# A linear-attention and sine-gated layer on one core: the opening with v in four loads, w1 issued behind them, and all v scaled by GpSimd

## The chip, the cores and the metric

One core of a Trainium2 chip runs the whole kernel. The metric is the device time in microseconds of one execution. Lower is better.

## The reference

Attention with a decay per head, over blocks, and then a two-layer network on the result (cut to what matters):

```python
# attention: q, k, v are [4, 8, 768, 64]; lam is [8]
for b in range(nb):                                  # blocks of 64 positions
    intra = einsum('bhic,bhjc->bhij', qb, kb) * Dmask        # lam**(i - j), i >= j
    intra = einsum('bhij,bhjd->bhid', intra, vb)
    inter = einsum('bhid,bhde->bhie', qb * lam_pow, kv_state)
    out[:, :, sl] = intra + inter
    kv_state = lam_block * kv_state + einsum('bhsd,bhse->bhde', kb * rev_pow, vb)

# network: x is the attention result as [3072, 512]
h = x @ w_in                                         # [3072, 2048]
g = h + sin(alpha * h)**2 / (alpha + 1e-9)
return g @ w_out                                     # [3072, 512]
```

## The kernel before

**Tiles and steps.** The kernel works on blocks of 128 positions. Two batch rows (`u` = 0, 1) share the 128 partitions, 64 each, and one step is one block of 128 positions of such a pair for four of the eight heads. There are 24 steps: two pairs of rows, 6 blocks and 2 halves of the heads. Steps 0 and 1 are the two head halves of block 0, steps 2 and 3 those of block 1. Four steps make 512 columns of x, one chunk of the network; there are six chunks.

**What one step does** (function `sec`). A step passes through three stages, each of which can be given to `sec` by the step's number:

- `t`: 32 TensorE transposes of q and k (L481) into PSUM, and one evacuation to `qkT` (L666) on the engine named in `t_engs`.
- `s`: 16 matmuls for the scores (L493), and their product with the causal mask into `S_m` (`put_S`, L611 on VectorE straight from PSUM; with `via`, ScalarE first copies the scores to `S_raw`, L607, and VectorE multiplies from there, L608).
- `o`: the output (L505 within the block, L515 with the state) and the state's increment (L528). `put_O` then evacuates the output times a decay table into `xT` (L624, VectorE), copies the first state for the next block to `Zs` (L634, ScalarE), and keeps the running state in `Zacc` (L629 the first time, L645 later).

The decay is carried by tables: v is scaled by `Lv` before use (`prep_v`, L460, v32 to v2, on GpSimd or VectorE), and x by `Xt` (L411) when it is evacuated.

**The network.** `grp_A` (L683) makes one 128-row slice of h for one chunk with four matmuls, ScalarE takes its sine (L687), one of three engines squares it (L694 or L695), and VectorE joins it with h into gT (L697). `grp_B` (L720) multiplies gT with w_out. Chunk 0's `grp_A` starts when x of steps 0 to 3 is complete; the attention of later steps is laid between the later matmuls.

**What sets the order.** The lines L758 to L895 record every operation with its engine and an estimated duration (`rec`, which is `Program.add`). The planner gives each one a start time: TensorE and SyncE in the order of recording, VectorE, ScalarE and GpSimd in the first gap that is long enough. DMA issues occupy their engine (0.75 us on GpSimd, less for small ones), and their landing is estimated from `nbytes`. Each engine then runs its operations in the order of these start times, and waits on semaphores for what they depend on. Readers of one PSUM bank on different engines are also put in the order of recording (L90 to L92). So a changed estimate can change an order, but not what is computed.

**The opening before.** k and q of blocks 0 and 1 are issued first (GpSimd, 8 loads of 128 KB). Then come transposes of steps 0 and 1, the mask tables (`consts2`), v of blocks 0 and 1 in eight loads of half the heads each (`by_step`, 128 KB), scores of steps 0 and 1, transposes of 2 and 3, and the scaling of step 0 on GpSimd. The first block of w1 is held back until that scaling is done. Then come scores of step 2, the scaling of step 1 on VectorE, the output of step 0 with the scores of step 3 ahead of its evacuation, the output of step 1, scalings of steps 2 and 3 on GpSimd, the last two w1 blocks behind them, and the outputs of steps 2 and 3. The Sin table load (L426) is recorded late, but the planner puts it in an early gap of ScalarE.

The PSUM banks of the opening: outputs of step 0 use banks 4 and 5, which its scores held, of step 1 banks 6 and 7, of steps 2 and 3 banks 0 to 3.

Of the kernel before, what the change touches and what calls it, by code (L numbers as in the profile page):

```python
# [187 lines left out]
def bass_lightning_attn__then__act_snake_kernel(  # L188
# [15 lines left out]
    NB = S // BL  # L204
# [5 lines left out]
    HS = 4  # L210
# [11 lines left out]
    with es:  # L222
        def sb(name, shape, dt):
            return es.enter_context(nc.sbuf_tensor(name, shape, dt))
# [28 lines left out]
        maskf = sb("maskf", [128, 256], F32)  # L253
# [6 lines left out]
        Lv = sb("Lv", [128, NB, H, 2], F32)  # L260
# [10 lines left out]
        junk = sb("junk", [128, 1], F32)  # L271
# [4 lines left out]
        P = Program()  # L276
# [19 lines left out]
        def half(r):  # L296
            return slice(64 * r, 64 * r + 64)

        def where(s):
            pair, n, hh = s // 12, (s % 12) // 2, s % 2  # L300
            return pair, n, hh

        def load(d, x, after=(), by_step=False, eng=None, us=(0, 1)):
            pair, n = d // NB, d % NB
            r = d % RL
            src, dst = {"k": (k, k2), "q": (q, q2), "v": (v, v32)}[x]
            ops = []
            for h0, h1 in ((0, HS), (HS, H)) if by_step else ((0, H),):
                for u in us:
                    a = bass.AP(src.tensor, ((2 * pair + u) * H + h0) * S * D + n * BL * D,  # L310
                                [[2 * D, 64], [S * D, h1 - h0], [1, 2 * D]])
                    keys = [f"{x}.{r}.{u}.{h // HS}" for h in range(h0, h1, HS)]
                    op = rec(eng or ("SP" if x == "v" else "POOL"),
                             lambda e, u=u, a=a, h0=h0, h1=h1: e.dma_start(dst[r][half(u), h0:h1, :], a), 0,  # L314
                             writes=keys, slot=f"{x}{r}{h0 if by_step else ''}{'p' if eng else ''}",
                             nbytes=(187000 if d < 2 else 150000) if x != "v" else 216500 // (2 if by_step else 1), after=after)
                ops.append(op)
            return ops if by_step else op

# [32 lines left out]
        def ident_op():  # L352
            rec("POOL", lambda e: e.affine_select(  # L353
                out=ident[:, :], in_=maskf[:, 0:128], pattern=[[-1, 128]], compare_op=ALU.not_equal, fill=1.0,
                base=0, channel_multiplier=1), 0.3, reads=["maskf"], writes=["ident"])
# [14 lines left out]
        def consts2():  # L370
            for u in range(2):
                op = rec("POOL", lambda e, u=u: e.affine_select(
                    out=mask2[u][:, :, :].rearrange("p a (b c) -> p a b c", b=2),
                    in_=maskf[:, :].rearrange("p (a b c) -> p a b c", a=2, b=2),
                    pattern=[[1, 2], [-1, 2], [-2, 64]], compare_op=ALU.is_gt, fill=1.0,
                    base=-128 * u, channel_multiplier=2), 0.3, reads=["maskf"], writes=[f"mask2.{u}"])
            for u in range(2):
                rec("DVE", lambda e, u=u: e.tensor_copy(mask[half(u), :, :], mask2[u][half(u), :, :]), 0.2,
                    reads=[f"mask2.{u}"], writes=[f"mask.{u}"])
            return op  # L380
# [41 lines left out]
                return last  # L422
            rec("PE", pe, 0.06 * n, reads=["maskf"], writes=bk(0))

        def sin_table():
            rec("ACT", lambda e: e.activation(junk[:, :], maskf[:, 0:1], ACTF.Sin), 1.5,  # L426
                reads=["maskf", "Lv"] + [f"X.{z}.{n}" for z in range(HS) for n in range(NB)], writes=["junk"])

        def alpha_ops(b):
            rec("PE", lambda e: e.transpose(PS[:, b, 0:NM], alpha_r[:, :], identf[0:NM, 0:NM]), 0.3,  # L430
# [8 lines left out]
        def w_load(fn, keys, slot, n, after):  # L439
            return rec("POOL", fn, 0, writes=keys, slot=slot, nbytes=131072 * n, after=after)  # L440

        def w1_block(m0, n, after=()):
            cs = slice(128 * m0, 128 * (m0 + n))
            src = moe_w_in[:, cs].rearrange("(c p) f -> p c f", p=128)
            return w_load(lambda e: e.dma_start(w1[:, :, cs], src), [f"w1.{m}" for m in range(m0, m0 + n)],
                          f"w1_{m0}", n, after)
# [6 lines left out]
        def prep_v(s, engs=("POOL", "DVE")):  # L453
            pair, n, hh = where(s)
            c, r = s % RC, s // 2 % RL
            src = v32[r][:, HS * hh:HS * hh + HS, :].rearrange("p h (t d) -> p (h t) d", t=2)
            L_b = bass.AP(Lv, (n * H + HS * hh) * 2, [[NB * H * 2, 128], [1, 2 * HS], [0, D]])
            reads, writes = part_keys("v", s) + ["Lv"], [f"v2.{c}"]
            eng, dur = fastest([(e, {"POOL": 1.05, "DVE": 0.65}[e]) for e in engs], reads, writes)
            rec(eng, lambda e: e.tensor_tensor(v2[c][:, :, :], src, L_b, ALU.mult), dur, reads=reads, writes=writes)  # L460
# [9 lines left out]
        def sec(t=None, o=None, s=None, tb=None, sb_=S_BK, ob=O_BK, peek=False, t_engs=("DVE", "ACT"), via=False, x_first=False, z_late=None, later=False):  # L470
            po, no, ho = where(o) if o is not None else (0, 0, 0)
# [102 lines left out]
            reads = []  # L574
# [14 lines left out]
            for seq, (_, keys, back) in zip(seqs, blocks):  # L589
# [3 lines left out]
                after = [done[back]] if back is not None and done[back] is not None else []  # L593
# [20 lines left out]
            def put_O(part=None):  # L614
                z = PS[:, ob:ob + 2, 256:384]
                acc = Zacc[ho]
                zs = Zs[o % 3][:, :, :, :].rearrange("p u a d -> p u (a d)")

                def put_x():
                    x, col = (o // 4) % NX, 256 * (no % 2)  # L620
                    xo = xT[x][:, 2 * ho:2 * ho + 2, col:col + 256].rearrange("p a (u i) -> p u a i", u=2)
                    xi = PS[:, ob:ob + 2, 0:256].rearrange("p u (a i) -> p u a i", a=2)
                    X_b = bass.AP(Xt, (2 * ho * NB + no) * 128, [[HS * NB * 128, 128], [0, 2], [NB * 128, 2], [1, 128]])
                    rec("DVE", lambda e: e.tensor_tensor(xo, xi, X_b, ALU.mult), 0.72,  # L624
                        reads=keys_o + [f"X.{2 * ho + a}.{no}" for a in range(2)],
                        writes=[f"x.{x}.{o % 4}"])

                def first_state():
                    rec("ACT", lambda e: e.copy(acc[:, :, :], z), 0.4, reads=keys_o, writes=[f"Zacc.{ho}"])  # L629

                if part != 1 and (no > 0 or o == 0):
                    put_x()
                if has_Z and no == 0:
                    rec("ACT", lambda e: e.copy(zs, z), 0.37, reads=keys_o, writes=[f"Zs.{o % 3}"])  # L634
                if no == 0 and o > 0:
                    put_x()
                if part == 0:
                    return
                if has_Z and no == 0:
                    if z_late is None:  # L640
                        first_state()
                    else:
                        z_late.append(first_state)
                elif has_Z:
                    rec("DVE", lambda e: e.tensor_tensor(acc[:, :, :], z, acc[:, :, :], ALU.add), 0.42,  # L645
                        reads=keys_o + [f"Zacc.{ho}"], writes=[f"Zacc.{ho}"])
                    rec("POOL", lambda e: e.tensor_copy(zs, acc[:, :, :]), 0.42,  # L647
                        reads=[f"Zacc.{ho}"], writes=[f"Zs.{o % 3}"])
# [8 lines left out]
            if t is not None:  # L657
# [4 lines left out]
                else:  # L662
                    ti = PS[:, tb[0]:tb[0] + 2, 0:256].bitcast(BF16)
                    to = qkT[j][:, :, :, :, :].rearrange("p u x a i -> p u (x a i)")
                eng, dur = fastest([(e, {"DVE": 0.7, "ACT": 1.05}[e]) for e in t_engs], keys_t, [f"qkT.{j}"])
                rec(eng, lambda e: (e.copy if eng == "ACT" else e.tensor_copy)(to, ti), dur,  # L666
                    reads=keys_t, writes=[f"qkT.{j}"])
# [96 lines left out]
        load(1, "k")  # L764
        load(1, "q")
        ident_op()
        sec(t=0, tb=(0, 1), t_engs=("DVE",))
        sec(t=1, tb=(2, 3), t_engs=("ACT",))
        consts2()
        clear_pads()  # L770
        load(0, "v", eng="POOL", by_step=True)
        load(1, "v", eng="POOL", by_step=True)
        identf_op()
        decay_table(0, 2)
        sec(s=0, sb_=4)
        sec(s=1, sb_=6)
        sec(t=2, tb=(0, 1), t_engs=("DVE",))
        sec(t=3, tb=(2, 3), t_engs=("ACT",))
        decay_table(2, NB)
        prep_v(0, ("POOL",))  # L780
        w1_block(0, 4, after=[P.ops[-1]])
        w1_block(4, 4)
        zl = []
        sec(s=2, sb_=0)
        prep_v(1, ("DVE",))
        o0 = sec(o=0, ob=4, z_late=zl, later=True)
        s3 = sec(s=3, sb_=2, via=True, later=True)
        s3()
        o0()
        sec(o=1, ob=6, z_late=zl)  # L790
        prep_v(2, ("POOL",))
        prep_v(3, ("POOL",))
        w1_block(8, 4, after=[P.ops[-1]])
        w1_block(12, 4)
        o2 = sec(o=2, ob=0, later=True)
        o3 = sec(o=3, ob=2, later=True)
        for f in o2, o3:
            f(0)
        for f in zl:
            f()  # L800
        sin_table()
        alpha_ops(4)
        for f in o2, o3:
            f(1)
# [125 lines left out]
```

## The time and the profile before

| | |
|---|---|
| median of 4 runs | 223.81 us (223.38 to 224.4) |
| the profiled execution | 223.75 us, of which the span is 221.9 |
| TensorE matmuls busy | 208.8 us, 94% of the span |
| VectorE busy | 146.6 us, 66% |
| ScalarE busy | 118.6 us, 53% |
| GpSimd busy | 96.9 us, 44% |
| first matmul of the network (L683) | 21.62 us after the span's start |
| mean granted TensorE clock | 0.959 of full speed |

The span is the time from the first to the last instruction that the profile shows; the other 1.85 us of the profiled execution lie around it. Busy shares are averages over stages that differ: in the first 21.6 us TensorE is often idle, and after that hardly ever. The DMA engines are busy from 3 to 15 us (k, q and v), nearly idle from 15 to 17, and busy again from 17 on (w1, then w2 and more).

### The profile page before, as it was taken

How to read it: one execution, taken by the hardware profiler on the slowest of the kernel's cores; microseconds unless marked ns; L12 is line 12 of the kernel's file. 1: busy time of each engine (PE TensorE's matmuls, PEld its weight loads, DVE VectorE, ACT ScalarE, POOL GpSimd, SP SyncE). 2: the span in 40 equal slices, each digit the busy share in tenths (PEclk: the TensorE clock that was granted, in tenths of full speed). 3: DMA queues.
4: the chain of work that ended last, by engine and by line, in shares of the span. 5: the costliest groups of instructions: out<-in, count | busy, mean ns of one | idle time of the engine just before them, and what ended most of it. 6: DMA issues, size and time to landing. Idle time of an engine off the chain costs nothing.

```text
span 221.9 us, 5711 instructions
## 1 busy us (share of the span) xinstructions
PE 208.8 (94%) x2457; PEld 106.0 (48%) x2457; DVE 146.6 (66%) x219; ACT 118.6 (53%) x193; POOL 96.9 (44%) x135
## 2 busy tenths in 40 slices
PE   7377999999999999999999999999999999999994
PEld 7254343455444454544455444455444545444453
DVE  2688499457479958498866688875578764477300
ACT  3853599240399924198923398702468321778030
POOL 7997991224446624033141431235464410555300
PEclk9855699999999999999999999999999999999999
DMA  6959999972879999869999998597910104102044
GB/s 64 156 168 181 194 188 199 245 136 28 114 132 237 217 137 177 191 132 141 217 138 203 160 136 181 118 110 185 158 33 17 35 0 104 41 0 48 2 95 95
DMA packets 62697, 28.37 MB, mean 128 GB/s; under 512 B 46656, under 2 KB 59216, under 8 KB 62672
## 3 DMA queue, kind: packets, MB, share of 16 engines
q0 software_dynamic: 30272, 12.59, 44.8%
q1 hardware_dynamic: 32144, 15.34, 33.0%
q8 instruction: 19, 0.31, 0.6%
q10 hardware_dynamic: 256, 0.08, 0.2%
q14 instruction: 6, 0.05, 0.1%
HBM read 27.28 MB, written 6.29 MB: 151 GB/s over the span
## 4 chain that ended last, share of the span: by engine, by line
PE 80%; DVE 9%; POOL 6%; ACT 2%; issue 1%; POOLq 0%; DVEq 0%
PE PS L720 35%; PE PS L683 32%; DVE gT L697 6%; PE PS L505 4%; PE PS L493 3%; PE PS L515 2%; POOL v L314 2%; PE PS L481 2%; DVE u L695 2%; PE PS L747 2%; PE PS L528 1%; POOL k L314 1%; POOL q L314 1%; DVE S_m L611 1%; ACT t L687 1%
## 5 line engine op out<-in xcount | busy, mean ns | idle before, releaser
L683 PE MATMUL PS<-xT,w 128*128 128x512 bf16 x384 | 88.7, 386 | 0.7 <-DVE xT L624 0.6
L720 PE MATMUL PS<-w,gT 128*128 128x512 bf16 x368 | 87.2, 380 | 0.0
L697 DVE SCALAR_TENSOR_TENSOR gT<-u,r_sb,PS 128x512 bf16<-128x512 bf16 x96 | 70.1, 746 | 17.9 <-POOL u L695 12.0
L687 ACT ACTIVATE t<-PS,alpha_sb 128x512 bf16<-128x512 f32 x96 | 63.0, 681 | 20.9 <-PE PS L683 20.5
L683 PEld LDWEIGHTS PS<-xT,w 128*128 128x128 bf16 x384 | 37.5, 99 | 48.5 <-issue 3.4
L720 PEld LDWEIGHTS PS<-w,gT 128*128 128x128 bf16 x368 | 33.9, 98 | 39.6
L611 DVE TENSOR_TENSOR S_m<-PS,mask 128x1024 bf16<-128x1024 f32 x23 | 28.1, 1223 | 20.8 <-PE PS L493 20.8
L727 ACT COPY osb<-PS 128x512 f32<-128x512 f32 x23 | 13.4, 582 | 49.5 <-PE PS L720 49.5
L460 POOL TENSOR_TENSOR v<-v,Lv 128x512 bf16<-128x512 f32 x17 | 18.4, 1095 | 39.7 <-DMA v<-in_v_dram 39.7
L695 POOL TENSOR_TENSOR u<-t 128x512 bf16<-128x512 bf16 x22 | 22.4, 1039 | 20.2 <-ACT t L687 20.2
L314 POOL DMA_DIRECT2D k<-in_k_dram x24 | 16.9, 711 | 23.7 <-PE PS L720 12.8
L694 ACT ACTIVATE u<-t 128x512 bf16<-128x512 bf16 x39 | 24.6, 630 | 1.7
L624 DVE TENSOR_TENSOR xT<-PS,Xt 128x512 bf16<-128x512 f32 x24 | 16.3, 683 | 9.1 <-PE PS L515 9.1
L695 DVE TENSOR_TENSOR u<-t 128x512 bf16<-128x512 bf16 x35 | 17.7, 506 | 5.7 <-ACT t L687 5.6
L314 POOL DMA_DIRECT2D q<-in_q_dram x24 | 16.5, 697 | 7.6 <-PE PS L720 4.4
L666 ACT COPY qkT<-PS 128x1024 bf16<-128x1024 bf16 x9 | 9.1, 1008 | 11.9 <-PE PS L481 9.2
L647 POOL CAST Zs<-Zacc 128x256 bf16<-128x256 f32 x16 | 7.1, 448 | 17.4 <-DVE Zacc L645 17.4
L505 PE MATMUL PS<-S_m,v 64*64 64x128 bf16 x384 | 11.4, 236 | 2.0 <-ACT Zs L634 0.9
L505 PEld LDWEIGHTS PS<-S_m,v 64*64 64x64 bf16 x384 | 7.3, 114 | 10.5 <-issue 6.4
L481 PE MATMUL PS<-ident,q 64*64 64x64 bf16 x192 | 6.3, 204 | 3.9 <-POOL ident L353 2.5
L528 PE MATMUL PS<-v,k 64*64 64x64 bf16 x320 | 8.8, 203 | 0.0
L481 PEld LDWEIGHTS PS<-ident,q 64*64 64x64 bf16 x192 | 4.4, 114 | 8.4 <-issue 5.9
(55 smaller groups left out, 124.1 us busy)
## 6 DMA issues: line engine op xcount, KB each, us to landing
out_dram<-osb SPq DMA_DIRECT2D x46, 128.0 KB, 2.6
v<-in_v_dram SPq DMA_DIRECT2D x16, 256.0 KB, 4.8
k<-in_k_dram POOLq DMA_DIRECT2D x24, 128.0 KB, 3.9
q<-in_q_dram POOLq DMA_DIRECT2D x24, 128.0 KB, 4.7
w<-in_moe_w_in_dram POOLq DMA_DIRECT2D x4, 512.0 KB, 7.3
w<-in_moe_w_out_dram POOLq DMA_DIRECT2D x4, 512.0 KB, 13.2
v<-in_v_dram POOLq DMA_DIRECT2D x8, 128.0 KB, 3.3
v<-in_v_dram POOLq DMA_DIRECT2D x4, 256.0 KB, 13.2
```

What stands on the lines that cost most here:

```text
L314: lambda e, u=u, a=a, h0=h0, h1=h1: e.dma_start(dst[r][half(u), h0:h1, :], a), 0,
L460: rec(eng, lambda e: e.tensor_tensor(v2[c][:, :, :], src, L_b, ALU.mult), dur, reads=reads, writes=writes)
L481: last = e.transpose(dst, part((q2, k2)[x], t, u, h, tt), ident[half(u), half(u)])
L505: return e.matmul(dst, v2[o % RC][half(u), hid(h, tj), :], S_part(o, u, h, tj), start=start, stop=True, skip_group_check=True)
L611: rec("DVE", lambda e: e.tensor_tensor(s_out, s_in, mask_b, ALU.mult), 1.25, reads=keys_s + ["mask.0", "mask.1"], writes=[f"S_m.{s % RS}"])
L624: rec("DVE", lambda e: e.tensor_tensor(xo, xi, X_b, ALU.mult), 0.72, reads=keys_o + [f"X.{2 * ho + a}.{no}" for a in range(2)], writes=[f" ...
L683: last = e.matmul(PS[:, i, :], w1[:, kc, 128 * m:128 * (m + 1)], xT[x][:, kc, :], start=(kc == 0), stop=(kc == NKC - 1))
L687: rec("ACT", lambda e: e.activation(t16[tt][:, :], PS[:, i, :], ACTF.Sin, scale=alpha_sb[:, m:m + 1]), 0.7, reads=bk(i) + ["alpha"], write ...
L694: return e.activation(u16[tt][:, :], t16[tt][:, :], ACTF.Square)
L695: return e.tensor_tensor(u16[tt][:, :], t16[tt][:, :], t16[tt][:, :], ALU.mult)
L697: rec("DVE", lambda e: e.scalar_tensor_tensor(out=gT[g][:, m, :], in0=u16[tt][:, :], scalar=r_sb[:, m:m + 1], in1=PS[:, i, :], op0=ALU.mul ...
L720: last = e.matmul(PS[:, bank, :], gT[g][:, m, 128 * s4:128 * (s4 + 1)], w2[:, m, :], start=(m == 0), stop=(m == NM - 1))
```

## The change

v of a block is loaded in two loads of 256 KB (one for each `u`, all eight heads) instead of four of 128 KB, and its size in the planner is set to 140000 for loads from GpSimd. The first two w1 blocks are recorded right behind the v loads and wait for nothing. The mask tables are recorded before the first transposes. The transposes of step 2 are evacuated by ScalarE and those of step 3 by VectorE. All four scalings of v are given to GpSimd. The Sin table load waits for the evacuation of step 2's transposes. The scores of step 3 come right behind those of step 2 and use the direct form of `put_S`, so `S_raw` is not used any more. The last two w1 blocks are recorded behind the scalings without a dependence on them. In `put_O`, x of step 0 is recorded behind the copy to `Zs`, as it is for step 1.

```diff
@@ load
-                             nbytes=(187000 if d < 2 else 150000) if x != "v" else 216500 // (2 if by_step else 1), after=after)
+                             nbytes=(187000 if d < 2 else 150000) if x != "v" else (216500 if eng is None else 140000), after=after)
@@
-        def sin_table():
+        def sin_table(after):
             rec("ACT", lambda e: e.activation(junk[:, :], maskf[:, 0:1], ACTF.Sin), 1.5,
-                reads=["maskf", "Lv"] + [f"X.{z}.{n}" for z in range(HS) for n in range(NB)], writes=["junk"])
+                reads=["maskf", "Lv"] + [f"X.{z}.{n}" for z in range(HS) for n in range(NB)], writes=["junk"], after=after)
@@ put_O
-                if part != 1 and (no > 0 or o == 0):
+                if part != 1 and no > 0:
                     put_x()
                 if has_Z and no == 0:
                     rec("ACT", lambda e: e.copy(zs, z), 0.37, reads=keys_o, writes=[f"Zs.{o % 3}"])
-                if no == 0 and o > 0:
+                if no == 0:
                     put_x()
@@ the opening
         ident_op()
+        consts2()
         sec(t=0, tb=(0, 1), t_engs=("DVE",))
         sec(t=1, tb=(2, 3), t_engs=("ACT",))
-        consts2()
         clear_pads()
-        load(0, "v", eng="POOL", by_step=True)
-        load(1, "v", eng="POOL", by_step=True)
+        load(0, "v", eng="POOL")
+        load(1, "v", eng="POOL")
+        w1_block(0, 4)
+        w1_block(4, 4)
         identf_op()
         decay_table(0, 2)
         sec(s=0, sb_=4)
         sec(s=1, sb_=6)
-        sec(t=2, tb=(0, 1), t_engs=("DVE",))
-        sec(t=3, tb=(2, 3), t_engs=("ACT",))
+        sec(t=2, tb=(0, 1), t_engs=("ACT",))
+        t2 = P.ops[-1]
+        sec(t=3, tb=(2, 3), t_engs=("DVE",))
+        prep_v(0, ("POOL",))
+        prep_v(1, ("POOL",))
         decay_table(2, NB)
-        prep_v(0, ("POOL",))
-        w1_block(0, 4, after=[P.ops[-1]])
-        w1_block(4, 4)
+        sin_table([t2])
         zl = []
         sec(s=2, sb_=0)
-        prep_v(1, ("DVE",))
-        o0 = sec(o=0, ob=4, z_late=zl, later=True)
-        s3 = sec(s=3, sb_=2, via=True, later=True)
-        s3()
-        o0()
-        sec(o=1, ob=6, z_late=zl)
+        sec(s=3, sb_=2)
         prep_v(2, ("POOL",))
         prep_v(3, ("POOL",))
-        w1_block(8, 4, after=[P.ops[-1]])
+        w1_block(8, 4)
         w1_block(12, 4)
+        sec(o=0, ob=4, z_late=zl)
+        sec(o=1, ob=6, z_late=zl)
         o2 = sec(o=2, ob=0, later=True)
         o3 = sec(o=3, ob=2, later=True)
         for f in o2, o3:
             f(0)
         for f in zl:
             f()
-        sin_table()
         alpha_ops(4)
```

## The prediction

> **What bounds the kernel now.** I read the chain of waits first, because a change of the opening is worth only what it moves the first matmul of the dense part (L683), then the order of time of GpSimd and VectorE over the first 22 us, then the landings of single v loads, and last the granted clock.
>
> The chain of waits, in order of time (start us, us, what):
>
> ```profile
> 8.62 4.99 POOL v L314 x8
> 13.61 0.10 POOL identf L390
> 13.71 1.04 POOL v L460
> 14.79 0.64 PE PS L505 x16
> ...
> 16.13 1.01 ACT S_raw L607
> 17.14 0.56 ACT Zs L634 x2
> ...
> 19.27 0.64 PE PS L505 x15
> ...
> 20.87 0.70 DVE xT L624
> 21.62 5.93 PE PS L683 x16
> 27.58 0.70 ACT t L687
> ```
>
> GpSimd issues v, scales step 0 from 13.71 to 14.75, the outputs of steps 0 to 3 follow, and their last evacuation xT releases L683 at 21.62. From there TensorE is nearly gapless (94% over the span), so a shift of 21.62 should show at the end.
>
> GpSimd's and VectorE's instructions in order of time (start, us, engine, line, operation):
>
> ```profile
> 15.04 1.56 POOL L445 DMA_DIRECT2D w<-in_moe_w_in_dram  x2 [0.30 <-POOL v L460]
> 16.59 2.07 POOL L460 TENSOR_TENSOR v<-v,Lv 128x512 bf16<-128x512 f32 x2
> ...
> 29.58 0.81 POOL L314 DMA_DIRECT2D v<-in_v_dram  x1
> ```
> ```profile
> 15.22 0.68 DVE L460 TENSOR_TENSOR v<-v,Lv 128x512 bf16<-128x512 f32 x1
> ...
> 17.17 2.05 DVE L608 TENSOR_TENSOR S_m<-S_raw,mask 128x1024 bf16<-128x1024 bf16 x1 [0.67 <-ACT S_raw L607]
> ```
>
> L608 is the surprise: the planner's cost for it is 0.6, it took 2.05 us, and it ended (19.22) 0.56 us after the two scalings beside it on GpSimd did (18.66). Step 3's output began 0.05 us later, at 19.27.
>
> The v loads (three answers, each of two neighbouring issues; the landing is counted from the start of the issue):
>
> ```profile
> L314 POOL DMA_DIRECT2D v<-in_v_dram x2: 676/678/679, 8.6 to 9.2; - x2
> ...
> DMA to landing us min/median/max: 3.3/3.8/4.4
> ...
> L314 POOL DMA_DIRECT2D v<-in_v_dram x2: 677/680/682, 9.9 to 10.5; - x2
> ...
> DMA to landing us min/median/max: 3.0/3.6/4.2
> ...
> L314 POOL DMA_DIRECT2D v<-in_v_dram x2: 699/702/704, 12.3 to 12.9; - x2
> ...
> DMA to landing us min/median/max: 3.0/3.2/3.4
> ```
>
> Issues start every 0.62 us from 8.62. The second landed at 9.24 + 4.4 = 13.64, the fourth at 10.48 + 4.2 = 14.7, the eighth at 12.94 + 3.4 = 16.3; the sixth, by the same view, took 4.0 and landed at 15.7. So step 0's half of block 0 (first two loads) was there just as GpSimd came free at 13.71, and all of block 0 a full us later. The loads were behind: each 256 KB took 1.06, 1.0 and 0.65 us, though GpSimd issued such a pair every 1.24.
>
> The granted clock, one stretch of 0.5 us:
>
> ```profile
> 26.00:26.50 0.50, 0.50 (x3) 0.12 (x2) 0.00 (x0) 0.50 (x1) 0.50 (x2) 0.71 1.26 209
> ```
>
> The clock is 0.50 from 9.3 until inside this stretch: the first 4.7 us of L683 run at half speed.
>
> **What the skill says.** "DMA: Bandwidth & Descriptors", "Why a DMA increments its semaphore by 16 and not by 1": up to 16 engines finish their shares independently, and only the full count means that all data landed. The same page, "Queues, rings and completion order": an engine takes its descriptors in ring order, so w1 behind v should not overtake it. The landings agree: a load counts when its slowest share is in, and these came at a steady pace of about 1 us per 256 KB however early they were issued. "SBUF — State Buffer", "Who interferes with whom": VectorE with two SBUF inputs fully blocks against a GpSimd instruction that reads SBUF; with one it doesn't. L608 (both inputs in SBUF) at 2.05 us agrees, and so does L611 (scores from PSUM), 1.22 us in three of three, one of them beside a scaling. "TensorE: Matmul & The Clock Gate", Part 1: the clock is released after a window of about 3.4 us of activity that doesn't start with the kernel; here 4.7 us, and no run shows the spread.
>
> **The change part by part.**
>
> *Mask copies first.* consts2 is recorded before the transposes. On GpSimd nothing moves; on VectorE the second mask copy (0.22 us) now goes ahead of qkT of step 0. Scores 0 come 0.23 later, S_m of steps 0 and 1 end at 12.95 instead of 12.73. Hidden: the next on VectorE, qkT of step 3, waits for transposes that end at 12.93. Without that cover it costs 0.2.
>
> *GpSimd's issues.* Four v loads for eight: 4 x 0.81 (the row at 29.58; bounds 0.68 as for a half load and 0.85 as at 31.7) = 3.24 for 4.99 us. Two w1 issues come in behind them, 1.56. Then identf. 8.62 + 3.24 + 1.56 + 0.19 = 13.6, as before (13.71): what the fewer loads save, the w1 issues take.
>
> *The scaling of step 0* needs both halves of both loads of block 0, so 512 KB instead of 256. Bounds: 13.6, GpSimd's own time, if larger loads land faster; 14.7, where 512 KB had landed before; up to 15.3 if the faster issue makes the engines' pace worse. I take 14.7, because the landings of before were paced by the slowest share and not by the issue. This is a new wait of 1.1 us, and it stands in GpSimd's order ahead of everything that follows: all four scalings, the other two w1 issues and aeps queue behind it, and TensorE's outputs wait for the scalings.
>
> *All scalings on GpSimd*, 1.04 each plus a 0.05 hand-over: 14.75 to 15.8, 16.85, 17.9, 18.95. Block 1 of v (16.3; 16.8 at an unchanged pace of 1.05 per 256 KB) just fits ahead of the third. VectorE loses its 0.68, which was on no path.
>
> *qkT of step 2 on ScalarE, of step 3 on VectorE, scores 2 and 3 together.* ScalarE is idle after 11.4 once the Sin table (1.28 + 0.20) is moved behind qkT: qkT of step 2 runs 12.55 to 13.55 (1.0), the table to 15.05, before Zs of step 0 at about 16.7. VectorE: qkT of step 3 12.95 to 13.65, L611 of steps 2 and 3 at 1.22 each, 14.3 to 16.75. So S_m of step 3 is there at 16.75 instead of 19.22, and S_raw (1.01 on ScalarE) and L608 go. That stall is gone; what is late next is the scaling.
>
> *Order of Zs and xT of step 0.* Readers of a bank are put in order by the planner; now Zs is ahead of xT. xT of step 0 waits for Zs and for L611: 17.1 to 17.8, needed only at L683.
>
> *The outputs.* Step 0: 15.8 to 16.65 (0.86 as before); Zs to 17.05. Step 1: 16.85 to 17.7; Zs to 18.1. Step 2 waits for its scaling, 17.9, and takes 1.55 (17.72 to 19.27 before): step 3 starts at 19.45, its scaling and S_m being there. As before xT starts 1.6 after that and L683 0.75 later: 19.45 + 1.6 + 0.75 = 21.8. Before it was 21.62: +0.2. A little less pace under the faster issue (0.1 on block 0, which moves all scalings) makes it 21.9, +0.3.
>
> *w1.* Blocks 0 and 1 are issued at 11.9 and 12.6 instead of 15.04 and 15.8. They land behind v: estimated at 512 KB per 2.5 us (205 GB/s, the rate while w1 flowed at 18 to 20 us) plus 1.3 from data to landing, block 0 by 19.5 to 20.5, so in time. Blocks 2 and 3 are issued at 18.95, as before. The idle stretch of the DMA engines at 15 to 17 us goes, which no engine waited for. In L683 and after, alpha (aeps on GpSimd) is as late as before, and the w2, k and q issues follow within 1 us of their old places. SP issues nothing in this stretch.
>
> Sum: 223.75 (profiled execution, span 221.9 and 1.85 around it) + 0.3 = 224.05. The median of the four runs is 0.06 above the profiled one: 224.1.
>
> **Rivals.** A difference under 0.5% (1.1 us) is what I call no change.
>
> *The v loads land early.* If 256 KB loads flow faster, block 0 is there at 13.6, step 2's scaling ends at 16.8, L683 starts at 20.7: -0.9, 222.9. For: the data ran at 249 GB/s over 10.5 to 13.0, with 0.2 us slices up to 307. Against: landings lagged the issue by over 4 us.
>
> *The v loads land late, slower than before.* Two loads' worth in flight at once, w1 queued behind, lengthen the slowest share. Each us by which block 1 is later than 16.8, or block 0 later than 14.7, is a us at L683. At 1.4 us per 256 KB from 13.64 on (1.0 measured) block 0 is in at 15.05 and block 1 at 17.85; the scaling of step 2 ends at 18.95, step 3's output starts at 20.55, L683 at 22.9: +1.3, 225.1. It decides "slower" from block 1 at 17.75 on. For: no slack is left, GpSimd has four scalings in a row and VectorE may not help. Against: the eight loads came at 1.0.
>
> *The clock decides.* If its release stays at 26.3, half of any shift is given back: 224.0. If it falls a window (3.4 us) earlier, the matmuls at half speed cost 1.7 us less: 222.4; a window later costs as much.
>
> **Chances.** Forecast, with the release fixed or not (223.7 to 224.7): 0.60. Early v: 0.14, about half beyond 0.5%. Late v: 0.18. Clock or a shifted order in the dense part: 0.08, both signs. That makes faster 0.12, same 0.66, slower 0.22. The range reaches from early v (222.9) to late v (225.1) and leaves about 2 in 10 outside.
>
> **What would show it.** Right: GpSimd idle before its first L460 until about 14.7, released by a v load; four L460 in a row, ending near 19; L611 four times at 1.22, no L608; step 3's L505 near 19.5; L683 first at 21.8 to 22. Wrong: L460 starting at 13.6 (early v), the third L460 waiting for a load (late v), L683 waiting for w, or the dense part from its first to last matmul changed by over 0.5 us.

## The result and the profile after

| | before | after |
|---|---|---|
| median of all runs | 224.28 us (63 runs) | 225.01 us (44 runs) |
| ratio to before, 95% interval | | 1.0036, 1.0021 to 1.0051 |
| profiled execution, its span | 223.75, 221.9 us | 224.85, 223.0 us |
| first L683 | 21.62 us | 21.89 us |
| its last instruction (L751) starts | 218.81 us | 219.91 us |

Some executions of each kernel fall in a slower state; the medians of this table count them, the ratio and its interval compare the fast ones alone. The first L683 is timed by its weight load, here and below, because some traces lack the record of the first matmul.

The change costs about 0.8 us (0.36% of 224), where 0.3 was forecast: within what was called no change, on its slow side. A second sample of the changed kernel, r1 below, gave 1.0019 (0.9987 to 1.0051).

The chain of waits after the change, in order of time (start us, us, what):

```profile
8.70 0.59 POOL v L314
9.29 5.34 DMA v<-in_v_dram
...
14.78 2.05 POOL v L460 x2
16.87 0.64 PE PS L505 x14
...
17.80 0.38 ACT Zs L634
...
18.25 0.64 PE PS L505 x14
...
19.77 0.42 PE PS L505 x13
...
21.14 0.70 DVE xT L624
21.89 5.96 PE PS L683 x16
```

Before, GpSimd's own issues led straight into the first scaling. Now a DMA stands between them: 5.34 us from the issue of block 0's second load to its landing at 14.6.

GpSimd in order of time after the change (start, us, engine, line, operation, and in brackets the idle time before it with what ended it):

```profile
8.60 2.79 POOL L314 DMA_DIRECT2D v<-in_v_dram  x4
11.32 1.62 POOL L445 DMA_DIRECT2D w<-in_moe_w_in_dram  x2
12.86 0.19 POOL L390 TENSOR_SCALAR_AFFINE_SELECT identf<-maskf 16x16 f32<-16x16 f32 x1
14.78 2.04 POOL L460 TENSOR_TENSOR v<-v,Lv 128x512 bf16<-128x512 f32 x2 [1.73 <-DMA v<-in_v_dram]
17.11 2.04 POOL L460 TENSOR_TENSOR v<-v,Lv 128x512 bf16<-128x512 f32 x2 [0.29 <-DMA v<-in_v_dram]
```

GpSimd is done with its issues at 13.05, then idles 1.73 us for block 0 and another 0.29 us, ahead of the third scaling, for block 1. VectorE at the same time:

```profile
14.29 2.36 DVE L611 TENSOR_TENSOR S_m<-PS,mask 128x1024 bf16<-128x1024 f32 x2 [0.64 <-PE PS L493]
17.21 0.69 DVE L624 TENSOR_TENSOR xT<-PS,Xt 128x512 bf16<-128x512 f32 x1 [0.56 <-ACT Zs L634]
```

Both masked scores are ready at 16.65, against 19.22 for step 3's before. That is 2.6 us gained off the path: nobody waits for them, since the scaling of step 2 ends only at 18.1. The answer for the last three v loads:

```profile
L314 POOL DMA_DIRECT2D v<-in_v_dram x3: 743/743/748, 9.3 to 10.6; - x3
...
DMA to landing us min/median/max: 5.3/5.3/6.4
```

The last load of block 1 was issued at 10.65 and landed 6.4 us later, at 17.05. The granted clock (the figure behind the busy times of the five engines):

```profile
26.50:27.00 0.50, 0.50 (x3) 0.23 (x2) 0.10 (x1) 0.37 (x1) 0.50 (x2) 0.89 1.01 109
```

It left 0.50 early in this stretch, at about 26.6; before, by the same reckoning from the 0.71 between 26.0 and 26.5, at about 26.3. In this pair the release so came 4.7 us after the first L683 both times, and nothing was gained or lost by it. Other executions differ in this ("The clock", below).

**Where the rest came from.** The opening is late by 0.27 us, and at 59 us the two traces are still only 0.33 us apart (the same instruction at 59.12 and 59.45). By the transposes behind the second run of L683 they are 1.18 us apart (78.61 and 79.79 in the chains), and at the end 1.10. So 0.85 us arises in one place, between 60 and 80 us. VectorE's squares (L695) there, before:

```profile
69.99 0.42 DVE L695 TENSOR_TENSOR u<-t 128x512 bf16<-128x512 bf16 x1
...
71.86 0.90 DVE L695 TENSOR_TENSOR u<-t 128x512 bf16<-128x512 bf16 x1
...
75.90 1.13 DVE L695 TENSOR_TENSOR u<-t 128x512 bf16<-128x512 bf16 x1
```

And after, with GpSimd's scalings of steps 8 to 11 in the fence behind it:

```profile
70.25 1.18 DVE L695 TENSOR_TENSOR u<-t 128x512 bf16<-128x512 bf16 x1
...
72.79 1.04 DVE L695 TENSOR_TENSOR u<-t 128x512 bf16<-128x512 bf16 x1
...
75.19 1.25 DVE L695 TENSOR_TENSOR u<-t 128x512 bf16<-128x512 bf16 x1
```
```profile
70.08 1.05 POOL L460 TENSOR_TENSOR v<-v,Lv 128x512 bf16<-128x512 f32 x1
...
72.47 1.06 POOL L460 TENSOR_TENSOR v<-v,Lv 128x512 bf16<-128x512 f32 x1
74.11 2.04 POOL L460 TENSOR_TENSOR v<-v,Lv 128x512 bf16<-128x512 f32 x2 [0.57 <-DMA v<-in_v_dram]
```

A square has both inputs in SBUF and takes 0.42 us alone. One that meets a scaling ends about 0.3 us behind it: 70.25 + 1.18 = 71.43 against 71.13 for the scaling, 75.19 + 1.25 = 76.44 against 76.15. By the same reading a scaling held L608 to 2.05 us before the change. "SBUF — State Buffer", "Who interferes with whom" in the Trainium skill gives the mechanism: VectorE with two SBUF inputs is blocked by a GpSimd instruction that reads SBUF. GpSimd before the change:

```profile
71.26 1.40 POOL L314 DMA_DIRECT2D q<-in_q_dram  x2
72.66 1.06 POOL L460 TENSOR_TENSOR v<-v,Lv 128x512 bf16<-128x512 f32 x1
75.70 2.22 POOL L460 TENSOR_TENSOR v<-v,Lv 128x512 bf16<-128x512 f32 x2 [1.98 <-DMA v<-in_v_dram]
```

The square of 1.13 at 75.90 lies beside a scaling in the same way. The one of 0.90 at 71.86 does not: it lies beside two issues of q loads and ends 0.1 us after the next scaling has begun. r1 and r2 below have one like it each (1.22 at 72.13, 0.90 at 73.08). With the scalings moved elsewhere (e3 and e4) all squares here take 0.42, those beside the q issues too, so it goes with the scalings; what held it is not shown.

Two squares were long before, at a cost of (0.90 - 0.42) + (1.13 - 0.42) = 1.19 us, and three after, at 0.76 + 0.62 + 0.83 = 2.21. The difference of 1.02 covers the 0.85.

### The profile page after: what moved, and what is told of

It is laid out like the page before. It is cut to its first block, busy times and chain, and to the rows that moved or that the text cites. A ratio compares the mean times of both kernels' runs of the same rounds, so it can differ in the third digit from the quotient of the medians.

```text
span 223.0 us, 5705 instructions
## 1 busy us (share of the span) xinstructions
PE 208.7 (94%) x2457; PEld 106.1 (48%) x2457; DVE 146.1 (66%) x218; ACT 117.8 (53%) x192; POOL 95.5 (43%) x132
## 4 chain that ended last, share of the span: by engine, by line
PE 80%; DVE 9%; POOL 4%; DMA 2%; ACT 1%; issue 1%; POOLq 0%; DVEq 0%
PE PS L720 35%; PE PS L683 31%; DVE gT L697 5%; PE PS L505 4%; PE PS L515 2%; DMA v<-in_v_dram 2%; PE PS L493 2%; DVE u L695 2%; PE PS L481 2%; PE PS L747 2%; PE PS L528 1%; POOL k L314 1%; POOL q L314 1%; POOL v L460 1%; ACT t L687 1%
## 5 line engine op out<-in xcount | busy, mean ns | idle before, releaser
L683 PE MATMUL PS<-xT,w 128*128 128x512 bf16 x384 | 88.8, 386 | 0.6 <-DVE xT L624 0.6
L720 PE MATMUL PS<-w,gT 128*128 128x512 bf16 x368 | 87.2, 380 | 0.0
L683 PEld LDWEIGHTS PS<-xT,w 128*128 128x128 bf16 x384 | 37.4, 99 | 48.5 <-issue 3.0
L720 PEld LDWEIGHTS PS<-w,gT 128*128 128x128 bf16 x368 | 33.8, 98 | 39.6
L611 DVE TENSOR_TENSOR S_m<-PS,mask 128x1024 bf16<-128x1024 f32 x24 | 29.2, 1222 | 20.9 <-PE PS L493 20.9
L460 POOL TENSOR_TENSOR v<-v,Lv 128x512 bf16<-128x512 f32 x18 | 19.0, 1067 | 39.6 <-DMA v<-in_v_dram 33.7
L695 POOL TENSOR_TENSOR u<-t 128x512 bf16<-128x512 bf16 x22 | 22.7, 1052 | 19.8 <-ACT t L687 19.8
L695 DVE TENSOR_TENSOR u<-t 128x512 bf16<-128x512 bf16 x35 | 18.5, 527 | 5.6 <-ACT t L687 5.5
```

The costliest lines, as they stand in the source:

```text
L611: rec("DVE", lambda e: e.tensor_tensor(s_out, s_in, mask_b, ALU.mult), 1.25, reads=keys_s + ["mask.0", "mask.1"], writes=[f"S_m.{s % RS}"])
L683: last = e.matmul(PS[:, i, :], w1[:, kc, 128 * m:128 * (m + 1)], xT[x][:, kc, :], start=(kc == 0), stop=(kc == NKC - 1))
L695: return e.tensor_tensor(u16[tt][:, :], t16[tt][:, :], t16[tt][:, :], ALU.mult)
L720: last = e.matmul(PS[:, bank, :], gT[g][:, m, 128 * s4:128 * (s4 + 1)], w2[:, m, :], start=(m == 0), stop=(m == NM - 1))
```

## The experiments

**1. w1 behind the scalings (e1).** The changed kernel, with the two w1 blocks taken from behind the v loads:

```diff
         load(1, "v", eng="POOL")
-        w1_block(0, 4)
-        w1_block(4, 4)
         identf_op()
@@
         prep_v(3, ("POOL",))
+        w1_block(0, 4, after=[P.ops[-1]])
+        w1_block(4, 4)
         w1_block(8, 4)
```

> The changed kernel with the first two w1 blocks issued behind the four scalings instead of right behind the v loads; all else in its order. If w1 in the queue slows the last v loads: the fourth v load, issued at 10.6, lands at 16.3 to 16.5 (as the last of the eight did before) instead of 17.0, and the third scaling starts at 16.85, straight behind the second, with no wait for v. If the pace is that of the v loads alone: the fourth lands at 17.0 again and the third scaling starts at 17.1. In both, w1 is issued from 19 on and lands about 5 us later, so L683 starts at 23.5 to 24.5 and the whole is 1.5 to 2.5 us slower than the changed kernel: that is the price of w1 and no answer to the question.

Measured: a single execution, 227.47 us, beside a median of 224.04 for the kernel before. GpSimd, the answer for the last three v loads, and TensorE's weight loads:

```profile
15.07 4.04 POOL L460 TENSOR_TENSOR v<-v,Lv 128x512 bf16<-128x512 f32 x4 [3.53 <-DMA v<-in_v_dram]
```
```profile
L314 POOL DMA_DIRECT2D v<-in_v_dram x3: 746/746/751, 9.3 to 10.7; - x3
...
DMA to landing us min/median/max: 5.1/5.6/5.6
```
```profile
24.95 0.13 PEld L683 LDWEIGHTS PS<-xT,w 128*128 128x128 bf16 x2 [3.81 <-DMA w<-in_moe_w_in_dram]
```

The last load lands after 5.6 us, at 16.3, instead of 17.05, and the third scaling waits for nothing. Counted from the landing of block 0 in the same profile, block 1 comes 1.4 us later here, and 2.4 us later in the changed kernel (2.2 and 2.1 in e3 and r1, which have the same loads). So w1 queued behind v delays the last of v by 0.7 to 1.0 us. Block 0 did not land earlier (first scaling 15.07 against 14.78), so its lateness isn't w1's doing. Held back this far, w1 becomes the wait itself (first L683 at 24.95, later than the 23.5 to 24.5 expected), and the time says nothing on the rest.

**2. Block 0 of v in halves again (e2).** The changed kernel with the old loads for block 0 alone:

```diff
-        load(0, "v", eng="POOL")
+        load(0, "v", eng="POOL", by_step=True)
```

> The changed kernel with block 0 of v in four loads of half the heads again (block 1 stays in two). GpSimd is busy with issues until about 14.3, and the first half of block 0 has landed by then. If the landing of block 0 sets the start of the network: all scalings come 0.45 earlier, L683 starts at 21.45 and the kernel is 0.4 us faster than the changed one. If block 1's landing sets it (third scaling at 17.1 waiting for v): the first scaling starts at 14.3, the third still at 17.1 or later, L683 stays at 21.8 to 22.0 and the time is that of the changed kernel within 0.2 us.

Measured: 224.57 us, ratio to before 1.0029 (1.001 to 1.0048). GpSimd:

```profile
14.13 2.05 POOL L460 TENSOR_TENSOR v<-v,Lv 128x512 bf16<-128x512 f32 x2
16.69 2.04 POOL L460 TENSOR_TENSOR v<-v,Lv 128x512 bf16<-128x512 f32 x2 [0.52 <-DMA v<-in_v_dram]
```

The first scaling comes 0.65 us earlier than in the changed kernel, the third only 0.42, since it waits for block 1; it came before the 17.1 that was expected for this case. Step 3's output began at 19.04 instead of 19.49, but a pause of TensorE of 0.38 us inside it, for which the trace names no releaser, and the first L683 at 22.05 left nothing of it. The squares between 60 and 80 us were held as in the changed kernel (1.11, 1.04 and 0.83). An early first scaling alone buys nothing while block 1 and four scalings in a row come behind.

**3. The scalings of steps 8 to 11 off the squares (e3, e4).** Squares lie in the runs of L683, none in the run of L720. The edit moves the four scalings into the L720 run of the same chunk, in the changed kernel (e3) and in the kernel before (e4):

```diff
-        AHEAD_A1 = {8: 8, 11: 9, 14: 10}
+        AHEAD_B1 = {0: 8, 1: 9, 2: 10, 3: 11}
@@ the run of L683
-                if c == 1 and m in AHEAD_A1:
-                    ahead(AHEAD_A1[m])
@@ the run of L720
+                if c == 1 and i in AHEAD_B1:
+                    prep_v(npr[0], ("POOL",), after=[op])
+                    npr[0] += 1
```

> The changed kernel with the scalings of steps 8 to 11 held back from the second run of L683 (64 to 77 us), where VectorE squares, to the first matmuls of L720 behind it. If the blocked squares (three of about 1.1 us instead of 0.42 in the changed kernel, two in the kernel before) carry what the opening does not explain: no L695 on VectorE over 0.5 us between 64 and 78, the profiled stretch from the first L683 of 64.5 to the first L611 after it shortens by 1.3 to 2 us, the kernel is 1 us or more faster than the changed one and stands 0.2 to 0.4 us behind the same edit of the kernel before. If the rest lies elsewhere (clock, order): the squares are free, but the time stays within 0.3 us of the changed kernel, and its distance to the same edit of the kernel before stays at 0.8 us.

> The kernel before with the same edit (scalings of steps 8 to 11 held back to the first L720 matmuls behind the second run of L683). Blocked squares: two of about 1 us become 0.42, 0.7 to 1.2 us faster than the kernel before (ratio 0.995 to 0.997). Rival (elsewhere): within 0.3 us of the kernel before.

Measured: e3 224.08 us, ratio to before 1.0001 (0.9983 to 1.0019); e4 223.66 us, 0.9985 (0.9967 to 1.0004). Every square between 60 and 78 us takes 0.42 or 0.43 in both; VectorE in e3:

```profile
70.65 0.42 DVE L695 TENSOR_TENSOR u<-t 128x512 bf16<-128x512 bf16 x1
...
72.47 0.42 DVE L695 TENSOR_TENSOR u<-t 128x512 bf16<-128x512 bf16 x1
...
74.28 0.42 DVE L695 TENSOR_TENSOR u<-t 128x512 bf16<-128x512 bf16 x1
```

So the scalings are what made the squares long. What this cost can be read at the first L611 behind this run, in the changed kernel and in e3:

```profile
81.00 1.23 DVE L611 TENSOR_TENSOR S_m<-PS,mask 128x1024 bf16<-128x1024 f32 x1 [1.35 <-PE PS L493]
```
```profile
80.05 1.23 DVE L611 TENSOR_TENSOR S_m<-PS,mask 128x1024 bf16<-128x1024 f32 x1 [1.94 <-PE PS L493]
```

From the same L683 (at 64.63 and 64.97) it is 16.37 us in the changed kernel and 15.08 in e3; 15.52 in the kernel before and 15.09 in e4; and 15.08 or 15.09 in every later profile with this edit. So the long squares cost 1.29 us of the profiled execution after the change and 0.43 before it, and the difference, 0.86, is the 0.85 that was to be explained. In r1 and r2 below (15.69 and 15.67) they cost 0.6 us each, with the change and without.

From the changed kernel to e3 the ratio falls by 0.35% (1.0036 to 1.0001), 0.8 us, or by 0.18% from its second sample; 1 us or more was expected. e4 gained 0.15% in this sample, half of the least that was expected, and its interval includes no gain. Without blocked squares the two kernels differ by 0.16% (1.0001 and 0.9985, with intervals that overlap): the size that was forecast for the opening, but not resolved. Run twice more, beside later kernels, e4 gave 0.9964 (0.9944 to 0.9984) and 0.9978 (0.996 to 0.9996).

**4. Both kernels again (r1, r2).** Without an edit.

> The changed kernel once more, for the spread of its opening and of its squares. If the surplus over the opening is a fixed effect: again three L695 on VectorE of over 0.8 us between 64 and 80, and a ratio to the kernel before near 1.0036. If it is chance of where the scalings of steps 8 to 11 fall: one or two such squares, and a ratio anywhere from 1.000 to 1.004. The opening: first L683 between 21.8 and 22.1.

> The kernel before once more, one look. First L683 between 21.6 and 22.1 if the 0.3 us between its profiled execution and that of its copy with moved scalings is a spread of the landings; VectorE's blocked squares two again if fixed, one to three if chance.

Measured: r1 224.43 us, ratio 1.0019 (0.9987 to 1.0051); r2, a single execution, 225.03. In r1 the changed kernel had two long squares (1.22 and 1.10), as r2 had (0.90 and 1.27): the third one is not a fixed property of the change. It came where v of steps 10 and 11 had landed early, with their scalings from 74.1 or 74.0 on (the changed kernel, e2); where they began at 75.7 to 77.1, behind a wait for v (the kernel before, r1, r2), two squares were long. The opening varies too, and neither first L683 fell where it was expected. The first scaling began at 13.70 and 14.61 in two profiles of the kernel before, at 14.78 and 15.74 in two of the changed one, the first L683 at 21.62 and 22.43, and 21.89 and 22.55.

**5. A better opening, first try (b1, b2).** The kernel before, with its v loads in halves, but w1 and the outputs rearranged and step 3's scores direct:

```diff
         prep_v(0, ("POOL",))
-        w1_block(0, 4, after=[P.ops[-1]])
-        w1_block(4, 4)
+        w1_block(0, 4)
+        prep_v(2, ("POOL",))
+        prep_v(3, ("POOL",))
         zl = []
         sec(s=2, sb_=0)
         prep_v(1, ("DVE",))
-        o0 = sec(o=0, ob=4, z_late=zl, later=True)
-        s3 = sec(s=3, sb_=2, via=True, later=True)
-        s3()
-        o0()
+        sec(s=3, sb_=2)
+        sec(o=0, ob=4, z_late=zl)
         sec(o=1, ob=6, z_late=zl)
-        prep_v(2, ("POOL",))
-        prep_v(3, ("POOL",))
-        w1_block(8, 4, after=[P.ops[-1]])
+        w1_block(4, 4)
+        w1_block(8, 4)
         w1_block(12, 4)
```

b2 is the same with the edit of e4.

> The kernel before with half loads kept, step 3's scores straight from PSUM (no S_raw, no L608), and only one w1 issue ahead of the scalings of steps 2 and 3 on GpSimd. If the opening is a chain of GpSimd work (issues and scalings) that ends in L683: third scaling starts at 15.9 instead of 16.6, step 3's output at 18.5 instead of 19.3, L683 at 20.9 to 21.1, ratio 0.996 to 0.998. If w1 is late instead: L683 waits for its first block, issued at 14.8 and landing 5.3 later, at 20.1 to 21.5, and little is won. If the clock's window takes it back: L683 early, but half of it lost by the first L720.

> The same opening with the scalings of steps 8 to 11 held back behind the second run of L683, as in the two kernels tried. If both effects are separate they add: 0.9 to 1.2 us faster than the kernel before (0.995 to 0.996). If the A run absorbs an earlier start (its squares bound it), no faster than the better of the two alone.

Measured: b1 224.64 us, ratio 1.001 (0.9974 to 1.0047); b2 223.76 us, 0.9981 (0.9937 to 1.0025); first L683 at 22.91 in b2's profile, where 20.9 to 21.1 was expected of this opening. VectorE in b2:

```profile
15.20 1.90 DVE L460 TENSOR_TENSOR v<-v,Lv 128x512 bf16<-128x512 f32 x1
17.02 1.21 DVE L611 TENSOR_TENSOR S_m<-PS,mask 128x1024 bf16<-128x1024 f32 x1
```

The scaling of step 1 on VectorE (0.68 us in the kernel before) has both inputs in SBUF and met GpSimd's scaling of step 2, which was put right there: 1.90 us, and all on VectorE behind it late. I had moved a second instruction into the same trap.

**6. Step 1's scaling ahead of the masked scores (b3).** b2 with two lines exchanged, so that VectorE scales step 1 while GpSimd issues w1:

```diff
-        sec(s=2, sb_=0)
         prep_v(1, ("DVE",))
+        sec(s=2, sb_=0)
         sec(s=3, sb_=2)
```

> The kernel before with v in halves, the first w1 block issued between the scalings of step 0 and 2 on GpSimd, steps 2 and 3 scaled by GpSimd right behind it, step 1 scaled by VectorE ahead of the masked scores of step 2 (in b1 it stood behind them, beside GpSimd's scaling of step 2, and took 1.89 us), and the scalings of steps 8 to 11 laid into the second half of the block of w_out matmuls as in e4. Theory (shared access of VectorE and GpSimd is what failed in b1): VectorE's scaling of step 1 waits for GpSimd's scaling of step 0 to end at about 14.8 and is over at about 15.5, inside GpSimd's issue of the w1 loads; masked scores of steps 2 and 3 end at 16.7 and 17.9, output of step 2 at 17.0, of step 3 at 18.2 to 18.6, first L683 at 20.9 to 21.3, ratio to the kernel before 0.995 to 0.998. Rival (the opening is set by something else, such as the landing of block 1's halves or TensorE's clock): L683 not before 21.6 even with step 3's output near 18.5, or the early start is given back by matmuls at a lower clock until 27, ratio 0.998 to 1.001, no better than e4.

> The same kernel as e4, beside b3 on the same chip: opening of the kernel before (first L683 between 21.6 and 22.4 by the landing of v), all squares of the second run of L683 at 0.42, ratio 0.997 to 1.000. If b3 is below it by 0.2% or more, the opening is worth something at the end; if they agree, what b3 gains before the first L683 does not arrive.

Measured: b3 223.48 us, ratio 0.9981 (0.9962 to 0.9999); e4 beside it 223.13 us, 0.9964, so b3's opening won nothing. Of VectorE and ScalarE in b3:

```profile
14.94 0.69 DVE L460 TENSOR_TENSOR v<-v,Lv 128x512 bf16<-128x512 f32 x1 [1.59 <-DMA v<-in_v_dram]
15.55 2.35 DVE L611 TENSOR_TENSOR S_m<-PS,mask 128x1024 bf16<-128x1024 f32 x2
17.81 1.28 DVE L624 TENSOR_TENSOR xT<-PS,Xt 128x512 bf16<-128x512 f32 x2
```
```profile
16.68 0.37 ACT L634 CAST Zs<-PS 128x256 bf16<-128x256 f32 x1 [2.70 <-PE PS L528]
18.52 0.37 ACT L634 CAST Zs<-PS 128x256 bf16<-128x256 f32 x1 [1.47 <-DVE xT L624]
```

The scaling is free of the stall, 0.69 us, and both masked scores are in at 17.9. But the first L683 came at 22.55, for a reason that neither theory had. The second Zs copy waited for an xT, which is queued on VectorE behind the masked scores, and step 2's output needs both Zs: it began at 18.95, not at 17.0. The kernel before records x of step 0 ahead of its Zs, which was harmless where xT of step 0 ran at 15.8, between step 1's scaling and L608.

**7. State first (b4).** b3 with the change's own edit of `put_O`:

```diff
-                if part != 1 and (no > 0 or o == 0):
+                if part != 1 and no > 0:
                     put_x()
@@
-                if no == 0 and o > 0:
+                if no == 0:
                     put_x()
```

> b3 with one edit more, the change's own in put_O: x of step 0 is recorded behind the copy to Zs. In b3 step 0's Zs waited for its xT, which stood behind both masked scores on VectorE, and step 2's output began at 18.95 instead of 17.0. Theory (that order was all that was late): both Zs copies done by about 17.1, output of step 2 at 17.1 to 17.3, of step 3 at 18.7 to 18.9, first L683 about 7.1 us after the first scaling begins (20.8 to 21.3 for a scaling at 13.7 to 14.2; the kernel before: 7.9 to 8.0), ratio to before 0.992 to 0.996. Rival (the gain before the first L683 is given back, to matmuls at a lower clock or to waits for w1): L683 early, but the time no better than e4's beside it, 0.996 to 1.000.

> The same kernel as e4 for a third time, beside b4 on the same chip: ratio 0.996 to 1.000 (0.9985 and 0.9964 so far). If b4 is 0.3 to 0.4% below it, the earlier L683 arrives at the end; if they agree within 0.2%, it is given back.

Measured: b4 221.96 us, ratio to before 0.9903 (0.9873 to 0.9932); e4 beside it 223.37 us, 0.9978 (0.996 to 0.9996). ScalarE, then VectorE, then TensorE's weight loads in b4:

```profile
15.80 0.37 ACT L634 CAST Zs<-PS 128x256 bf16<-128x256 f32 x1 [2.02 <-PE PS L528]
16.44 0.37 ACT L634 CAST Zs<-PS 128x256 bf16<-128x256 f32 x1 [0.27 <-PE PS L528]
```
```profile
14.72 0.69 DVE L460 TENSOR_TENSOR v<-v,Lv 128x512 bf16<-128x512 f32 x1 [1.41 <-DMA v<-in_v_dram]
15.32 2.35 DVE L611 TENSOR_TENSOR S_m<-PS,mask 128x1024 bf16<-128x1024 f32 x2
17.59 1.88 DVE L624 TENSOR_TENSOR xT<-PS,Xt 128x512 bf16<-128x512 f32 x3
```
```profile
20.39 0.13 PEld L683 LDWEIGHTS PS<-xT,w 128*128 128x128 bf16 x2 [0.68 <-DVE xT L624]
```

Both Zs copies now wait for TensorE alone, step 2's output begins at 16.83, and the first L683 at 20.39: 1.2 us before that of the kernel before, and 2.2 before b3's, of which 0.25 is an earlier landing of v (first scaling at 13.77 and 14.02). b4's interval lies wholly below e4's beside it, by 0.75% in the middle (0.9903 and 0.9978), and below the 0.992 to 0.996 expected. So the gain reaches the end. It is more than the 1.2 us of the opening (0.54%), and where the rest comes from stays open. The interval rests on six executions, each shorter than the one before it (223.09 down to 221.01); why stays open too.

The profile alone wouldn't show the gain. It is of the longest of the six executions, and beside the third e4 it has the first L683 1.2 us earlier, but also an earlier release of the clock (at 26.0 and at 27.5). The same L683 starts at 58.30 and 59.61, the last L751 at 218.14 and 218.83.

## Why the prediction was right, and where it was off

**GpSimd's issues.** Off by size, without effect. The v loads took GpSimd 0.70 us each (2.79 for four), near the lower bound of 0.68 and not 0.81, so GpSimd was free at 13.05 instead of 13.6. It then waited for data, so the half microsecond was worth nothing.

**The scaling of step 0.** Right: 14.78 for a forecast of 14.75, released by a v load. r1 against r2 has the same step one landing later: 15.74 and 14.61. Waiting for 512 KB instead of 256 cost 1.08 us in the first pair and 1.13 in the second. Two of the figures behind it were read loosely: the data ran at 256 GB/s over 10.5 to 13.0, not at 249, and the "steady pace" of 1 us per 256 KB leaves out the last pair of loads, which took 0.65.

**"Block 1 just fits".** Off by size. It landed at 17.05, not at 16.3 to 16.8, and the third scaling waited 0.29 us, which I had listed as a sign of the late rival. e1 shows the missing term: w1 in the queue behind it, 0.7 to 1.0 us (16.3 without). I had reckoned that w1 would follow v and leave its pace alone. The rival's threshold of 17.75 for "slower" was not reached.

**The scalings in a row, and the outputs.** The last scaling ended at 19.15 (18.95 forecast), step 2's output began at 18.25 (17.9), held by Zs of step 1 at 18.17 as much as by its scaling at 18.1. Step 3's began at 19.49 (19.45), since step 2's took 1.24 us to the start of the next instead of the 1.55 I carried over from before. Two misses of 0.3 us cancelled by luck, and L683 at 21.89 fell on the forecast of 21.8 to 21.9. Between other profiles the step is smaller: 22.43 to 22.55 (r2, r1) and 22.02 to 22.03 (e4, e3), so its +0.27 is known no better than to some 0.3.

**The stall goes, and what is late next.** Right. No L608, masked scores at 16.65, and the four scalings on GpSimd became the path. That is why removing a 2.05 us stall brought nothing.

**"Zs ahead of xT".** I saw the order and priced it at nothing. For the changed kernel that left the sum right, but it misses what the edit is worth where masked scores of two steps stand together on VectorE: b3 and b4 differ in it alone, and step 2's output begins at 18.95 and 16.83.

**The clock.** Here the agreement of the profiled pair is luck. The last rival holds in this, that part of a shift of the release, near a half, shows in the time: the kernel before and two profiles of e4 (the second and the third) have the same opening, and the first L683 at 21.62, 21.60 and 21.59. Before, the release came at 26.3. In the second e4 the clock is full from 25.0 on:

```profile
24.00:25.00 1.00, 1.00 (x4) 0.31 (x3) 0.66 (x2) 0.28 (x1) 1.00 (x3) 0.50 1.22 197
25.00:26.00 1.00, 1.00 (x6) 0.49 (x5) 0.52 (x1) 0.76 (x2) 1.00 (x2) 1.00 1.21 195
```

In the third, whose trace has no earlier record of the clock, the matmuls of L683 stand 0.43 us apart until 27.5 and 0.22 after that. The same L683 behind them starts at 59.12, 58.50 and 59.61. Over the profiles of all kernels this change of spacing comes 3.3 to 6.0 us after the first L683, in no order by kernel (3.3 in r1, 5.5 in r2). So single executions can lie over 1 us apart by the clock alone, more than three times the 0.3 that was forecast. That the two profiled ones had the same 4.7 is chance, as far as these runs show; a median over many executions depends less on it.

**"Rest after L683 unchanged".** This is the step that failed in the profiled pair: from the first L683 to the last instruction the changed kernel took 0.83 us longer (198.02 against 197.19). The mechanism was quoted for L608, and not looked for at the squares, where the trace of before already had two at 0.90 and 1.13 among others at 0.42. With them gone (e3) the changed kernel is at 1.0001, not 1.0036. The clock is no rival for this pair, with 4.7 us to its release in both. That the change itself brings the third blocked square isn't shown, as r1 had two.

**The size.** Forecast +0.3 us (0.13%); 0.36% in the first sample lies above it with its whole interval, 0.19% in the second includes it. The opening accounts for the forecast part; the squares, where the profile shows the remainder, vary between executions.

## What to carry to other kernels

Removing a stall pays only as far as the next input of the same consumer: here masked scores came 2.6 us earlier and then waited for scalings that the same change had put in one queue, behind larger loads with w1 behind them. When VectorE and GpSimd share SBUF, place VectorE's instructions with two SBUF inputs against GpSimd's DMA issues rather than its arithmetic (with the exception above: three squares were long beside issues that stood between two scalings), and look for the pattern along the whole trace, since one short instruction at two durations gives it away. When an evacuation is put in order with a copy on another engine, let the one that TensorE waits for go first. And before two single profiles are compared, see whether their clock was released at the same distance from the start of the dense part.

## What the runs showed of the hardware beyond expectation

A square that meets a GpSimd scaling ends a fixed time behind it, 0.28 to 0.30 us in eleven squares between 60 and 80 us (the changed kernel, before, r1, r2, e1, e2). So the price is what is left of the GpSimd instruction, less about 0.1 us. In the changed kernel the square at 70.25 had 0.88 us of a scaling still before it and took 0.76 more than alone; the one at 72.79 had 0.74 and took 0.62 more. Squares went from 0.42 to between 0.90 and 1.27 us over four profiles, and a 128x512 scaling on VectorE from 0.68 to 1.90. Against that, 150 squares that met DMA issues alone took 0.41 to 0.43 us. L611, with the scores in PSUM, stayed near 1.2 us beside scalings (2.36 for two in the changed kernel).

The same collision comes twice more in the kernel before, and in e3 and e4 too, where VectorE's squares meet squares on GpSimd (1.17 at 165.59 and 1.24 at 197.16 before). There it seems to cost nothing: matmuls are busy for 79.94 us of the 80 from 120 to 200.

A load of 256 KB took 4.4 to 6.4 us from issue to landing (4.6 to 7.1 in r1) with three others in flight and w1 behind it, and 4.2 to 5.6 without w1; the loads of 128 KB before the change took 3.0 to 4.4. Two loads share a semaphore here, so the landing of the first of a pair, and with it the lower figures, is an assignment; that of the second isn't. The same kernel's landings moved by 0.9 us from one profile to another (first scaling at 13.70 and 14.61), and the release of its clock by over 2 us against the first L683 (3.4 to 6.0 us behind it, kernel before and e4); each is larger than the difference that was to be predicted.
